# Moving the turned dV and dK tiles and the W_down^T loads on the DMA queue of a fused attention and GLU backward kernel

## The chip, the cores and the metric

The kernel runs on one core of a Trainium2 chip. Its engines are PE (TensorE, with its weight loads shown apart as PEld), DVE (VectorE), ACT (ScalarE), POOL (GpSimd) and SP (SyncE). SP does nothing here but issue DMAs, one after the other, and waits in front of each for what that DMA needs; POOL issues DMAs too, beside some arithmetic. The metric is the device time of one execution in microseconds; the figure for a kernel is the median of its runs.

## The reference

The layer is y = x + s * silu(g). With xn the layer norm of x (2048 x 576, bfloat16), s is an attention block with given keys and values, and g is a gated MLP:

```python
q = (xn @ wq).reshape(B, Sq, H, Dh)                    # H = 32 heads of Dh = 128
p = softmax(q k^T * Dh**-0.5);  o = p @ v;  s = o @ wo # Sk = 2048
h = sigmoid(xn @ w_gate) * (xn @ w_up)                 # F = 4608
g = h @ w_down
```

The kernel returns the output and the gradients of x, k, v, wq, wo, w_gate, w_up and w_down for a given grad_out. The gradients of k and v are 32 matrices of 2048 x 128 each, and those are the tiles that this change is about.

## The kernel before

The program is one straight line of stages. P is 128, NT = 16 row tiles of x, DT = 5 column tiles of D = 576 (four of 128 and one of 64).

1. Layer norm and the products with w_gate and w_up. The rows a, b and h (sigmoid, its derivative's factor, the hidden row) go to DRAM as a_d, b_d, h_d. Then h @ w_down.
2. The heads, 32 of them, to about 3610 us. Their order is written out by hand with positions. dV and dK of a head come out transposed, as 128 x 2048, and go to DRAM as dvT_d and dkT_d in pieces of 128 x 512.
3. The product of the attention rows with wo (L852), 16 row tiles. Its left operand oT is loaded and transposed by DMA into five buffers, oT0 to oT4. In its second half five pieces of W_down^T are loaded (`load_wdT`, L836), the first of three thirds: wdT0. doB and doBT, what flows back into the MLP, are made here.
4. The dh stage (L870 to L961), 18 blocks of 256 columns of F, counted by fb from 0. A block needs h_blk, a_blk and b_blk, 1024 KB each; `load_abh` (L878) loads them, two blocks ahead, into two sets of buffers: a_blk and b_blk on SP, h_blk on POOL except in block 0, where it goes on SP too. PE makes dh (L905, `make_dh`), ACT copies it out (dhc, three buffers), DVE multiplies it with a_blk and b_blk into du_blk and dg_blk, POOL stores these to DRAM, and PE goes on with dW_down (L923, `make_dwd`), then dW_up and dW_gate (L947) and the remainder of their columns (L955). Blocks 0 to 9 also load one of the ten pieces of the second and third thirds of W_down^T (wdT1, used from block 6; wdT2, used from block 12).
5. The dWo stage (L970 to L1034), eight groups of four heads (hg): dWo (L1005) from onb and ds_all, dWq (L1014, L1023) from dqb and xn_all. `load_hg` loads onb and dqb two groups ahead. `wT_loads` brings W_up^T and W_gate^T by transposing DMAs, two per group in the first five groups.
6. The last stage (L1039 to L1099), eight parts of 256 rows, counted by sbi from 0: dxn from eight passes over du, dg and dq, each loaded and transposed by DMA into cf and cq buffers (L1061), then the layer norm's backward and dx. In the last part the two dx stores are SP's, in the others POOL's.

Turning dV and dK back is spread over stages 4 to 6. The list `turns` has 64 entries, dK and dV of each head. A turn loads one 128 x 2048 matrix by a transposing DMA into a buffer named turn and stores it, 512 KB, to the output later. `turn(pool, n)` (L151) first issues the stores of all tiles loaded by the call before, then the loads of n new ones:

```python
def turn(pool, n):
    while turned:
        nc.sync.dma_start(*turned.pop(0))
    for _ in range(n):
        if turns:
            src, dst = turns.pop(0)
            t_ = pool.tile([P, NT, P], bf, name="turn")
            nc.sync.dma_start_transpose(t_[:], src)
```

Each of the three stages has its own pool of two turn buffers (4096 bytes per partition each). The dh stage turns two tiles at the end of each block (36), the dWo stage two at the end of each group (16), the last stage one at passes 1, 4 and 7 of the parts after part 0 as long as there are any: 12, the last one in part 4.

In stages 4 to 6 SP's order is the program's own (`manual_schedule`); PE, DVE, ACT and POOL are ordered by the scheduler. A DMA on SP stands behind everything that SP issues before it, and behind the wait of each of those. A buffer waits for whatever lay in the same bytes before: the pools are stacked, and the memory of one stage is that of the stage before it.

Of the kernel before, what the change touches and what calls it, by code (L numbers as in the profile page):

```python
# [9 lines left out]
bf = mybir.dt.bfloat16  # L10
# [3 lines left out]
P = 128  # L14
# [81 lines left out]
def kernel(  # L96
# [6 lines left out]
    nc = tc.nc  # L103
# [6 lines left out]
    NT = S // P  # L110
# [40 lines left out]
    def turn(pool, n):  # L151
        while turned:
            nc.sync.dma_start(*turned.pop(0))
        for _ in range(n):
            if turns:
                src, dst = turns.pop(0)
                t_ = pool.tile([P, NT, P], bf, name="turn")
                nc.sync.dma_start_transpose(t_[:], src)
                turned.append((dst, t_[:]))

# [628 lines left out]
    if True:  # L789
# [80 lines left out]
        with tc.tile_pool(name="b1o", bufs=2, reuse_waits="tile") as outp, tc.tile_pool(name="b1k", bufs=2, reuse_waits="tile") as tkp, tc.tile_pool(name="b1t", bufs=3, reuse_waits="tile") as tmpp, \  # L870
# [21 lines left out]
            for fb in range(F // FB):  # L892
                fcols = slice(fb * FB, (fb + 1) * FB)
# [44 lines left out]
                load_abh(fb + 2)  # L938
                if fb < DT * (NWD - 1):
                    load_wdT(fb % DT, 1 + fb // DT)  # L940
                turn(tkp, 2)
# [19 lines left out]
            turn(tkp, 0)  # L961
# [8 lines left out]
        with tc.tile_pool(name="c2b", bufs=1, reuse_waits="tile") as blk, tc.tile_pool(name="c2s", bufs=2, reuse_waits="tile") as sb, \  # L970
# [26 lines left out]
            for hg in range(NHG):  # L997
                cols = slice(hg * HG * P, (hg + 1) * HG * P)
                onb, dqb = held.pop(hg)
                for hl in range(HG):  # L1000
                    h = hg * HG + hl
                    accs = [ps.tile([P, 512], f32, name=f"acc{j}") for j in range(len(ncs))]
                    for st in range(NT):
                        for j, (n0, nn) in enumerate(ncs):
                            nc.tensor.matmul(accs[j][:, :nn], lhsT=onb[:, st, hl * P:(hl + 1) * P], rhs=ds_all[:, st, n0:n0 + nn],  # L1005
                                             start=(st == 0), stop=(st == NT - 1))
                    dwo = sb.tile([P, D], bf, name="dwo")
                    for j, (n0, nn) in enumerate(ncs):
                        alt.copy(dwo[:, n0:n0 + nn], accs[j][:, :nn])
                    nc.gpsimd.dma_start(out_5[h * P:(h + 1) * P, :], dwo[:])  # L1010
# [22 lines left out]
                turn(tkp, 2)  # L1033
            turn(tkp, 0)  # L1034
# [4 lines left out]
        with tc.tile_pool(name="c4c", bufs=1, reuse_waits="tile") as chp, tc.tile_pool(name="c4s", bufs=2, reuse_waits="tile") as sb, \  # L1039
# [11 lines left out]
            for sbi in range(S // SB2):  # L1051
# [7 lines left out]
                for pi, (src_d, wT, k0, KC, nm) in enumerate(passes):  # L1059
                    ch = chp.tile([P, KC, SB2], bf, name=f"cq{pi % 2}" if nm == "cq" else f"cf{pi % 3}")  # L1060
                    nc.sync.dma_start_transpose(ch[:], src_d[scol, k0 * P:(k0 + KC) * P])  # L1061
                    if sbi == 0 and pi in (1, 3, 4, 6):
                        load_wqT((1, 3, 4, 6).index(pi))
                    elif sbi and pi % 3 == 1:
                        turn(tkp, 1)
# [33 lines left out]
            turn(tkp, 0)  # L1099
# [33 lines left out]
```

## Time and profile before

| what | us |
|---|---|
| median of three runs | 5088.66 (5080.39 to 5103.23) |
| the profiled execution | 5100.3 |
| its span, first to last instruction | 5098.5 |
| PE busy in it | 4977.9 (98%) |
| the dh stage: first product of L905 to the last of L947 | 3801.5 to 4407 |
| the dWo stage: first product of L1005 | 4422.5 |
| the last stage: first product of L1072 | 4675.9 |

Lines such as "PE dh L905 <- DMA wdT<-in_B_w_down_dram: 7.9, 1, 7.9" give who waited at which line, what ended the wait, the total in microseconds, how often and the longest. "SPq" is SP's own queue of instructions, "L158 DMA_TRANSPOSE turn<-dkT_d" the issue of one DMA there. A chain or timeline line begins with its start and its length in microseconds; the length of an SP issue is how long SP was held by it, and not the transfer, whose end is its landing. A line of stretches ends with the granted share of PE's clock, the mean busy share of the 16 DMA engines (it can pass 1, since packets of two queues overlap) and GB/s.

### The profile page before, as it was taken

How to read it: one execution, taken by the hardware profiler on the slowest of the kernel's cores; microseconds unless marked ns; L12 is line 12 of the kernel's file. 1: busy time of each engine (PE TensorE's matmuls, PEld its weight loads, DVE VectorE, ACT ScalarE, POOL GpSimd, SP SyncE). 2: the span in 40 equal slices, each digit the busy share in tenths (PEclk: the TensorE clock that was granted, in tenths of full speed). 3: DMA queues.
4: the chain of work that ended last, by engine and by line, in shares of the span. 5: the costliest groups of instructions: out<-in, count | busy, mean ns of one | idle time of the engine just before them, and what ended most of it. 6: DMA issues, size and time to landing. Idle time of an engine off the chain costs nothing.

```text
span 5098.5 us, 103815 instructions
## 1 busy us (share of the span) xinstructions
PE 4977.9 (98%) x43024; PEld 3071.8 (60%) x43024; DVE 3087.7 (61%) x4821; ACT 2435.7 (48%) x3131; POOL 1484.0 (29%) x2197
## 2 busy tenths in 40 slices
PE   9999999999999999999999999999899999899999
PEld 3344666666666666666666666666457777654554
DVE  6556778878887887887888788777432222110101
ACT  5533656666666676666666667666202122100000
POOL 4322323333333333233333323322223223211000
PEclk9999999999999999999999999999999999999999
DMA  7889999999999999999999999999999999999995
GB/s 260 265 206 167 197 198 201 198 197 200 202 200 203 203 201 204 202 203 202 199 200 200 205 204 197 199 199 203 189 235 262 230 244 252 282 278 254 207 198 119
DMA packets 2855051, 1079.04 MB, mean 212 GB/s; under 512 B 2659889, under 2 KB 2782769, under 8 KB 2854577
## 3 DMA queue, kind: packets, MB, share of 16 engines
q1 hardware_dynamic: 2769312, 786.61, 87.3%
q0 software_dynamic: 85264, 285.79, 19.8%
q8 instruction: 336, 5.51, 0.4%
q14 instruction: 139, 1.13, 0.1%
HBM read 172.54 MB, written 234.55 MB: 80 GB/s over the span
## 4 chain that ended last, share of the span: by engine, by line
PE 86%; DMA 8%; issue 2%; DVE 2%; ACT 1%; POOL 1%; SPq 0%; DVEq 0%; POOLq 0%; ACTq 0%
PE acc L612 16%; PE acckv L630 15%; PE sp L552 8%; PE acc L1072 8%; PE dp L582 7%; PE accp L511 5%; PE accw L947 4%; DMA dST<-dSq 4%; PE dh L905 3%; PE acc L392 3%; PE accd L923 3%; PE acc L1005 3%; PE acc L852 2%; PE accq L1014 2%; PE acct L518 2%
## 5 line engine op out<-in xcount | busy, mean ns | idle before, releaser
L563 ACT ACTIVATE Pq<-sneg,nm 128x2048 bf16<-128x2048 bf16 x512 | 1025.0, 2002 | 182.6 <-DVE sneg L554 181.6
L585 DVE SCALAR_TENSOR_TENSOR dSq<-dp,delta,Pq 128x1024 bf16<-128x1024 f32 x608 | 774.9, 1282 | 445.9 <-PE dp L582 442.9
L612 PE MATMUL acc<-Kn,dST 128*128 128x128 bf16 x8192 | 977.0, 219 | 36.9 <-DMA dST<-dSq 36.2
L612 PEld LDWEIGHTS <-dST 128*128 128x128 bf16 x8192 | 692.3, 98 | 464.7 <-DMA dST<-dSq 57.6
L612 PE MATMUL acc<-Vn,PT 128*128 128x128 bf16 x8192 | 948.8, 219 | 11.7 <-DMA PT<-Pq 11.6
L612 PEld LDWEIGHTS <-PT 128*128 128x128 bf16 x8192 | 682.7, 98 | 428.8 <-DMA PT<-Pq 18.6
L630 PE MATMUL acckv<-Pq,dOn 128*128 128x512 bf16 x2048 | 762.9, 380 | 0.0
L630 PE MATMUL acckv<-dSq,Qn 128*128 128x512 bf16 x2048 | 758.9, 379 | 0.0
L554 DVE TENSOR_SCALAR_CACHE_REDUCE sneg<-sp,nm 128x1024 bf16<-128x1024 f32 x512 | 657.0, 1283 | 97.6 <-PE sp L552 64.8
L554 DVE TENSOR_SCALAR_CACHE_REDUCE sneg<-sp 128x1024 bf16<-128x1024 f32 x512 | 625.2, 1221 | 92.2 <-PE sp L552 82.8
L588 ACT ACTIVATE t<-dp,negdelta 128x1024 bf16<-128x1024 f32 x416 | 464.8, 1117 | 426.0 <-PE dp L582 324.5
L552 PE MATMUL sp<-KT,QT 128*128 128x512 bf16 x2048 | 610.5, 380 | 7.3 <-DVE sneg L554 7.0
L582 PE MATMUL dp<-VT,dOT 128*128 128x512 bf16 x2048 | 609.9, 379 | 0.6 <-DVE dSq L585 0.5
L592 DVE TENSOR_TENSOR dSq<-t,Pq 128x1024 bf16<-128x1024 bf16 x416 | 307.3, 739 | 0.0
L571 POOL TENSOR_TENSOR dOn<-dOn,rinv_all 128x256 bf16<-128x256 bf16 x256 | 153.8, 610 | 491.6 <-DVE dOn L42 305.4
L630 PEld LDWEIGHTS <-dOn 128*128 128x128 bf16 x2048 | 200.5, 98 | 74.5 <-issue 0.4
L630 PEld LDWEIGHTS <-Qn 128*128 128x128 bf16 x2048 | 200.5, 98 | 73.8
L511 PE MATMUL accp<-xnT,wq_h 128*128 128x512 bf16 x640 | 240.9, 381 | 2.8 <-ACT xnT L40 0.8
L947 PEld LDWEIGHTS <-xn_all 128*128 128x128 bf16 x2304 | 224.2, 98 | 27.8
L1085 DVE SCALAR_TENSOR_TENSOR junk<-dxn,xn_all 128x576 f32<-128x576 f32 x16 | 12.1, 758 | 369.3 <-ACT dxn L1080 369.3
L676 POOL DMA_DIRECT2D dq_d<-dq_n x128 | 99.1, 774 | 456.6 <-DVE dq_n L675 419.4
L1072 PEld LDWEIGHTS <-cf 128*128 128x128 bf16 x2304 | 146.3, 98 | 141.3 <-DMA cf<-dg_d 3.8
(186 smaller groups left out, 7059.2 us busy)
## 6 DMA issues: line engine op xcount, KB each, us to landing
out_dram<-turn SPq DMA_DIRECT2D x64, 512.0 KB, 4.9
h_d<-h_row POOLq DMA_DIRECT2D x48, 384.0 KB, 3.0
a_d<-a_row POOLq DMA_DIRECT2D x48, 384.0 KB, 3.5
b_d<-b_row POOLq DMA_DIRECT2D x48, 384.0 KB, 4.5
a_blk<-a_d SPq DMA_DIRECT2D x18, 1024.0 KB, 8.3
b_blk<-b_d SPq DMA_DIRECT2D x18, 1024.0 KB, 21.4
du_d<-du_blk POOLq DMA_DIRECT2D x18, 1024.0 KB, 9.6
dg_d<-dg_blk POOLq DMA_DIRECT2D x18, 1024.0 KB, 12.5
```

The source lines that it names most:

```text
L511: nc.tensor.matmul(acc[:], lhsT=w[:, i, :], rhs=(srcT if i < DL else xnT)[:, i, cs], start=(i == 0), stop=(i == DL))
L552: nc.tensor.matmul(sp[:, c * CH:(c + 1) * CH], lhsT=hs.QT[:, qs], rhs=hs.KT[:, hf * HW_ + c * CH: hf * HW_ + (c + 1) * CH], start=True, st ...
L554: nc.vector.tensor_scalar(sneg[:, hf * HW_:(hf + 1) * HW_], sp[:], -SCALE, None if hf == 0 else nm[:, hf - 1:hf], op0=ALU.mult, op1=ALU.mi ...
L563: nc.scalar.activation(Pq[:], sneg[:], AF.Exp, bias=nm[:, hf:hf + 1], scale=-1.0, accum_out=hs.rs_all[:, qt:qt + 1])
L582: nc.tensor.matmul(dp[:, c * CH:(c + 1) * CH], lhsT=hs.dOT[:, qs], rhs=hs.VT[:, hf * HW_ + c * CH: hf * HW_ + (c + 1) * CH], start=True, s ...
L585: nc.vector.scalar_tensor_tensor(dSq[:, hsl], dp[:], hs.delta[:, qt:qt + 1], Pq[:, hsl], op0=ALU.subtract, op1=ALU.mult)
L588: nc.scalar.activation(t[:], dp[:], AF.Identity, bias=hs.negdelta[:, qt:qt + 1], scale=1.0)
L592: nc.vector.tensor_tensor(dSq[:, hsl], t[:], Pq[:, hsl], op=ALU.mult)
L612: nc.tensor.matmul(bx.acc[:, j, :], lhsT=T[qt][:, kt, :], rhs=getattr(hs, rhs)[:, kt, :], start=(kt == 0), stop=(kt == NT - 1))
L630: nc.tensor.matmul(bx.acc[i][:], lhsT=getattr(hs, rhs)[:, qt, :], rhs=slabs[qt][:, k0:k0 + CH], start=(qt == 0), stop=(qt == NT - 1))
L947: nc.tensor.matmul(acc[:kd, :FB], lhsT=xn_all[:, st, d0:d0 + kd], rhs=blk_[:, st, :], start=(st == 0), stop=(st == NT - 1))
L1072: nc.tensor.matmul(accs[sl][j][:, :nn], lhsT=ch[:, kk, sl * P:(sl + 1) * P], rhs=w_[:, n0:n0 + nn], start=(pi == 0 and kk == 0), stop=(las ...
```

## The change

`turn` now loads at most one tile per call, and issues the load before the stores of what the call before loaded, so that a store stands one call, and one load, later on the queue. The calls are spread anew:

- dh stage: one at the end of each block, and one more at the start of each odd block: 27 tiles. The pool has three buffers instead of two.
- dWo stage: one at the end of each group and one after the products of each group's first head: 16 tiles as before.
- last stage: as before one at passes 1, 4 and 7 of parts 1 to 7, now used to the end: 21 tiles. The store of the last one follows the two dx stores on SP.

In the dh stage the piece of W_down^T goes on SP's queue before a_blk and b_blk of two blocks on, no longer behind them. Nothing in the heads, and no arithmetic, is changed.

```diff
--- before.py
+++ after.py
@@ -148,16 +148,15 @@
     turns = [(src[h], out[0, h].rearrange("(p t) d -> p t d", t=NT)) for h in range(H) for src, out in ((dkT_d, out_2), (dvT_d, out_3))]
     turned = []
 
-    def turn(pool, n):
-        while turned:
-            nc.sync.dma_start(*turned.pop(0))
-        for _ in range(n):
-            if turns:
-                src, dst = turns.pop(0)
-                t_ = pool.tile([P, NT, P], bf, name="turn")
-                nc.sync.dma_start_transpose(t_[:], src)
-                turned.append((dst, t_[:]))
-
+    def turn(pool, load=True):
+        old, turned[:] = list(turned), []
+        if load and turns:
+            src, dst = turns.pop(0)
+            t_ = pool.tile([P, NT, P], bf, name="turn")
+            nc.sync.dma_start_transpose(t_[:], src)
+            turned.append((dst, t_[:]))
+        for (dst, t_) in old:
+            nc.sync.dma_start(dst, t_)
 
     pers = ctx.enter_context(tc.tile_pool(name="pers", bufs=1))
     ident = pers.tile([P, P], bf, name="ident")
@@ -867,7 +866,7 @@
         pc = tc.alloc_tile_pool(name="pc", bufs=1, side="right", reuse_waits="tile")
         xn_all = pc.tile([P, NT, D], bf, name="xn_all")
         FB = min(256, F)
-        with tc.tile_pool(name="b1o", bufs=2, reuse_waits="tile") as outp, tc.tile_pool(name="b1k", bufs=2, reuse_waits="tile") as tkp, tc.tile_pool(name="b1t", bufs=3, reuse_waits="tile") as tmpp, \
+        with tc.tile_pool(name="b1o", bufs=2, reuse_waits="tile") as outp, tc.tile_pool(name="b1k", bufs=3, reuse_waits="tile") as tkp, tc.tile_pool(name="b1t", bufs=3, reuse_waits="tile") as tmpp, \
                 tc.tile_pool(name="b1r", bufs=2, reuse_waits="tile") as dblk, \
                 tc.tile_pool(name="b1l", bufs=1, reuse_waits="tile") as ldp, \
                 tc.tile_pool(name="b1ps", bufs=2, space=PSUM, reuse_waits="tile") as ps, \
@@ -890,6 +889,8 @@
             nc.sync.dma_start(xn_all[:], xn_d[:, :].rearrange("(t p) d -> p t d", p=P))
             load_abh(1)
             for fb in range(F // FB):
+                if fb % 2:
+                    turn(tkp)
                 fcols = slice(fb * FB, (fb + 1) * FB)
                 fh = slice(fb * FB % FH, fb * FB % FH + FB)
                 h_blk, a_blk, b_blk = blks.pop(fb)
@@ -935,10 +936,10 @@
                     make_dh()
                     for fl in range(FB // P):
                         make_dwd(fl)
-                load_abh(fb + 2)
                 if fb < DT * (NWD - 1):
                     load_wdT(fb % DT, 1 + fb // DT)
-                turn(tkp, 2)
+                load_abh(fb + 2)
+                turn(tkp)
                 for (blk_, out_, nm) in ((du_blk, out_7, "dwu"), (dg_blk, out_6, "dwg")):
                     stg_ = outp.tile([P, DL, FB], bf, name=nm)
                     for i, (d0, kd) in enumerate(dts[:DL]):
@@ -958,7 +959,7 @@
                 alt.copy(dwl[:], acc[:, :FB])
                 for k, out_ in enumerate((out_7, out_6)):
                     nc.gpsimd.dma_start(out_[D - KL:, fcols], dwl[k * KL:(k + 1) * KL, :])
-            turn(tkp, 0)
+            turn(tkp, False)
         pcw.release()
         pc2.release()
 
@@ -1004,6 +1005,8 @@
                         for j, (n0, nn) in enumerate(ncs):
                             nc.tensor.matmul(accs[j][:, :nn], lhsT=onb[:, st, hl * P:(hl + 1) * P], rhs=ds_all[:, st, n0:n0 + nn],
                                              start=(st == 0), stop=(st == NT - 1))
+                    if hl == 0:
+                        turn(tkp)
                     dwo = sb.tile([P, D], bf, name="dwo")
                     for j, (n0, nn) in enumerate(ncs):
                         alt.copy(dwo[:, n0:n0 + nn], accs[j][:, :nn])
@@ -1030,8 +1033,8 @@
                 load_hg(hg + 2)
                 for (dst, src, d0, kd) in wT_loads[2 * hg:2 * hg + 2]:
                     nc.sync.dma_start_transpose(dst[:, :, d0:d0 + kd], src[d0:d0 + kd, :])
-                turn(tkp, 2)
-            turn(tkp, 0)
+                turn(tkp)
+            turn(tkp, False)
 
         SB2 = min(256, S)
         FC = ldiv(FT, 12)
@@ -1062,7 +1065,7 @@
                     if sbi == 0 and pi in (1, 3, 4, 6):
                         load_wqT((1, 3, 4, 6).index(pi))
                     elif sbi and pi % 3 == 1:
-                        turn(tkp, 1)
+                        turn(tkp)
                     last = pi == len(passes) - 1
                     for kk, sl in ([(kk, sl) for sl in range(nsl) for kk in range(KC)] if last else
                                    [(kk, sl) for kk in range(KC) for sl in range(nsl)]):
@@ -1096,7 +1099,7 @@
                     dx = sb.tile([P, D], bf, name="dx")
                     nc.vector.tensor_tensor(dx[:], t2[:], got[:], op=ALU.add)
                     (nc.sync if sbi == NSB - 1 else nc.gpsimd).dma_start(o1[rows, :], dx[:])
-            turn(tkp, 0)
+            turn(tkp, False)
             assert not turns
         pc3.release()
         pc.release()
```

## The prediction

> **What bounds the kernel now.** I read the page first, then PE's waits in the stages after the heads, then the chain in order of time, then the SyncE queue's (SP's) timeline around each wait, and last the busy time by stretch. The heads, up to about 3610 us, are not touched, so only what follows them is priced.
>
> The page's first lines and PE's waits (stretches 3780:4400, 4400:4600 and 4600:4780; total us, times, longest):
>
> ```profile
> span 5098.5 us, 103815 instructions
> PE 4977.9 (98%) x43024; PEld 3071.8 (60%) x43024; DVE 3087.7 (61%) x4821; ACT 2435.7 (48%) x3131; POOL 1484.0 (29%) x2197
> PE dh L905 <- ACT dhc L909: 8.6, 3, 7.7
> PE dh L905 <- DMA wdT<-in_B_w_down_dram: 7.9, 1, 7.9
> PE acc L1005 <- DMA onb<-on_d: 13.0, 1, 13.0
> PE acc L1072 <- DMA cf<-dg_d: 3.5, 1, 3.5
> PE acc L1072 <- DMA cq<-dq_d: 2.1, 1, 2.1
> ```
>
> PE is the bound; only its few waits can be won, and all of them end on a transfer that SP issues. The chain around them (start us, us, what):
>
> ```profile
> 3966.56 8.84 PE dh L905 x80
> ...
> 3982.07 25.37 DMA wdT<-in_B_w_down_dram
> 4007.49 11.13 PE dh L905 x76
> ...
> 4124.66 27.21 DMA b_blk<-b_d
> 4153.14 4.99 PE dh L905 x30
> 4158.13 7.84 PE accd L923 x64
> ...
> 4406.82 15.60 DMA onb<-on_d
> 4422.47 17.57 PE acc L1005 x128
> ```
>
> A dh block takes PE 32.5 us (3836.48 to 3869.00). Block 6 should have begun at 3966.56+32.52 = 3999.08 and its dh ended at 4007.9; it ended at 4018.62: **10.7 us lost**, 7.9 of waiting and the rest at a slow clock (granted 0.84 over 3999:4031.5). Block 10's dh should have ended at 4148.8 (4107.40+32.52+8.84) and ended at 4158.13: **9.4 lost**. The dWo stage could have begun at 4393.61+13.97+1.87 = 4409.5; it began at 4422.47 and its first product took 17.57 instead of 15.79: **14.8 lost**. SP's timeline just before (start, us):
>
> ```profile
> 3783.31 0.38 SPq L885 DMA_DIRECT2D h_blk<-h_d  x1
> 3801.15 0.37 SPq L885 DMA_DIRECT2D a_blk<-a_d  x1
> ...
> 3948.47 13.21 SPq L158 DMA_TRANSPOSE turn<-dkT_d  x1
> 3961.72 16.56 SPq L158 DMA_TRANSPOSE turn<-dvT_d  x1
> ...
> 4402.33 3.66 SPq L153 DMA_DIRECT2D out_dram<-turn  x2
> 4406.23 0.38 SPq L994 DMA_DIRECT2D ds_all<-ds_d  x1
> ```
>
> The W_down^T piece and b_blk are late because SP was held by turns; ds_all and onb are late because the last turns end at 4406. SP's own waits add "SPq L158 <- DMA out_dram<-turn: 132.1, 24, 18.0": a load waiting for the store of the same buffer, issued just before it. But the DMA share is 1.0 to 1.2 over the whole dh stage, so much of this wait is real traffic and not free time.
>
> **The change part by part.**
>
> *Fewer tiles in the dh stage (36 to 27).* Price of a tile, load and store: the last stage shows a DMA share of 1.01 in 4829:4880 with three tiles and 0.68 in 4982:5033 with none; 0.33 of 51 us over 3 is 5.6 us. Low end: a_blk and b_blk of block 0, issued together, reached DVE 4.0 us apart (its first products with them begin at 3808.59 and 3812.57), so 1 MB is 4.0 us, and a tile moves 1 MB. High end: the pair at 3948 held SP for 30 us, 15 each. I take 5.6, the one row in which nothing but the tiles differs.
>
> *Block 6.* Its last W_down^T piece landed at 4007.45. In the changed order 6 loads and 5 stores stand ahead of it instead of 8 and 6: about 1.5 tiles, -8.4 us. It also goes ahead of a and b of its block, -8.0. Added: 4.0 for an h_blk that moves into this stage (below). It lands near 3995 against a need at 3999.1+3.9. The 10.7 go. If tiles are 4.0 it lands at 3997.
>
> *Block 10.* Its b_blk landed at 4151.87. Ahead of it now stand 12 loads and 11 stores instead of 16 and 14, 3.5 tiles, -19.6. But one more W_down^T piece is now ahead: low 1.5 us (the shortest issue), high 7.9 (the median), and I take 4.9, its median landing of 10.5 less the 5.6 of the shortest. And the h_blk of block 0 adds 4.0. So 4151.9-19.6+4.9+4.0 = 4141.2. PE comes to block 10 at 4129.2+3.9 and can go some 4 us without b (three dhc buffers and two in PSUM), to 4137.1. Some 4 us late, and 2 for the slow clock: 6 of the 9.4 stay, **3.4 won**. From block 11 no W_down^T piece is left, and SP gains.
>
> *The third turn buffer.* It is 4096 bytes per partition, and everything allocated above it moves up. In the built program h_blk of block 0 then lies on oT0, which the last product of the stage before (L852, to about 3801.1) still reads. Before, h_blk was issued at 3783.31 and only a_blk waited for that. Now h, a and b all go after 3801.1. With h first, b comes one transfer (4.0) and one issue (0.4) later. PE reached the first product of L947 8.1 us after b (3812.35 to 3820.48); of the dwd products that stand between, 25 instead of 29 are left then, 0.5 us less: **+3.9**. Low end 0 (h hidden under the first dh blocks), high end 12, were h to hold b up by the 21.4 us less 10.8 that b's median landing has over this one. SP, ACT and POOL queue behind it, and all move by as much.
>
> *Start of the dWo stage.* After the last a/b loads only 4 loads and 5 stores are left instead of 6 and 6. Before, a of block 17 went at 4350 and SP was free at 4406. Two tiles less are 11 us, and in the seven blocks from 11 on, half a tile less per block brings SP forward by 2.8 each: it is free near 4375 for ds_all. onb waits for PE's last dwd, 15.8 us before the stage ends; its median landing is 11.1, so it is there. Late next is dqb: it waits for the dwl stores and was issued at 4415.78, 6.3 us after PE's end; it is needed 15.8 after, and takes 8.5 (the shortest) to 13.6 (the median). Price 0 to 4, I take 1, for ds_all and onb no longer run beside it. The new turn behind it on SP waits for PE's accl only, long ended. **-13.8**.
>
> *In the dWo stage* the number stays 16; one tile moves to the stage's head, and a load waits for the store issued one step before it, as now. SP's cover is its waits on PE (29.9 us at L992 in all). 0, between -2 and +2.
>
> *The last stage (12 to 21).* The nine tiles fall into parts 5 to 7. Parts 1 to 4 carry the same three per part with PE at 51.00 of 51:
>
> ```profile
> 4829.00:4880.00 51.00, 51.00 (x418) 26.21 (x416) 6.30 (x16) 1.78 (x8) 2.15 (x4) 1.00 1.01 207
> 4982.00:5033.00 51.00, 51.00 (x419) 26.46 (x418) 6.29 (x16) 1.78 (x8) 2.15 (x4) 1.00 0.68 147
> ```
>
> The cover is SP's slack on PE, 10.7 us in the first of these stretches and 21.2 in the second. 0 on PE; without the cover a late cf costs 3.5 and, as at onb, about 2 of slow clock. The last store, though, now stands behind the two dx stores: the last dx issue begins at 5095.63 and lands 1.8 later; the turn's store is issued 0.33 behind it and takes 2.8 (the shortest) to 4.9 (the median): +1.3 to +3.4. Nothing else is in flight then, so I take the low end: **+1.4**.
>
> **Sum.** 3.9-10.7-3.4-13.8+1.4 = **-22.6 us**. The profiled execution took 5100.3 (span 5098.5 and 1.8 around it): 5077.7. It is 11.6 above the median of the three runs, 5088.66; the same difference on the median gives **5066.1**, -0.44%.
>
> One rule makes the tiles cheaper. The Trainium skill, page "Advanced Engine Details and Errata", section "X-Bar Transpose (TRN2)", says that transposing transfers are as fast as plain ones. By it a tile would be 4.0 us (an estimate from a and b above) and a W_down^T piece of 0.375 MB 1.5: block 10 then comes 5.6 less 3.4, some 2.2 us, later than priced, and the sum would be -20.4. The trace's windows (5.6) disagree.
>
> **The rivals.**
>
> *Both dh waits go and block 10 is free* (the queue is the limit, not the engines: 132.1 us of SP's waits fall away). For it: a_blk lands in 6.2 us at its best and 24.2 at its worst, the same megabyte, by what POOL's du, dg and h do beside it. Against: the DMA share never falls below 0.97 there, so a transfer moved is a transfer somewhere else. It gives 6 us more: 5060.1. A rule beside it: "DMA: Bandwidth & Descriptors", section "Queues, rings and completion order" of the Trainium skill, says that each DMA engine takes turns between the queue rows that have work; a tile less on SP's row would then free more than its own time while POOL's row is full. The trace's 6.2 to 24.2 us agree with it.
>
> *The traffic stays in the way*: turns that meet POOL's three 1 MB transfers are slow whatever their number (12 to 17 us each at 3948 and again at 4262, against a median of 2.6). Then blocks 6 and 10 lose what they lose now: 14.1 more, 5080.2. Against: fewer turns meet them.
>
> *Slower than before*: the nine late tiles hold cf or cq back. If each costs 3.5+2 us, that is 49.5: 5115.6. It decides once SP's 10.7 us of slack per part are used up; the parts that carry three tiles now speak against it.
>
> **How the numbers follow.** Forecast 0.42 (its own range 5060 to 5073), block 10 free 0.26, traffic stays 0.23, slower 0.09. The range takes in the first three with the ends of the unknown costs (start to +12, dqb 3, clock): 5050 to 5092. A measurement of this kernel can tell about 0.5% from no change, here 25.4 us. Below 5063.2 lie nearly all of the second case and a quarter of the first: 0.34; above 5114 most of the last: 0.08; between, 0.58.
>
> **What would show it.** In the profile after: PE's wait on wdT gone and onb's gone or under 2; a wait of a few us on dhc or b_blk near block 10; h_blk of block 0 issued by SP after the last L852 product instead of 18 us before, and PE idle some 4 us there; ds_all issued before PE's last dwd; parts 5 to 7 of the last stage at a DMA share near 1 with PE full; a turn store as the last transfer. I am wrong if the dh stage has new waits on a_blk or wdT, if dqb waits for more than 3 us, or if cf does after part 4.

## The result, and the profile after

The changed kernel takes 5123.01 us (median of 20 runs, 5098.3 to 5165.2) against 5104.43 for the kernel before (20 runs beside them): the ratio is 1.0046, 95% interval 1.0024 to 1.0068. It is slower by a little under half a per cent, where 5066 and a small gain had been forecast. A later comparison on another chip gave 1.0027 (1.0002 to 1.0052).

The page of the profiled execution (5136.24 us) begins:

```profile
span 5134.5 us, 103068 instructions
PE 4950.8 (96%) x42270; PEld 3077.3 (60%) x43024; DVE 3088.9 (60%) x4821; ACT 2437.8 (47%) x3131; POOL 1483.9 (29%) x2197
```

PE's waits of the changed kernel, first over the dh stage (3826:4460), then up to the first parts of the last stage (4460:4780); total us, times, longest:

```profile
PE dh L906 <- issue: 16.7, 3, 8.5
PE dh L906 <- ACT dhc L910: 3.6, 2, 3.4
PE accd L924 <- DMA h_blk<-h_d: 3.6, 1, 3.6
PE accd L924 <- issue: 2.9, 3, 1.4
...
PE acc L1075 <- DMA cf<-dg_d: 5.6, 2, 4.8
PE acc L1075 <- DMA cf<-du_d: 5.5, 2, 3.6
```

The rows that were to go are gone: no wait on wdT in the dh stage, none on onb at the start of the dWo stage. New are 16.7 us of "issue" in the dh product (PE stands and nothing that the profile follows holds it), 2.9 more in dwd, and 11 us on cf where there were 3.5. The chain of the changed kernel shows the places:

```profile
4096.85 7.40 issue
4104.25 9.24 PE dh L906 x69
...
4186.97 22.95 DMA b_blk<-b_d
4211.19 6.09 PE dh L906 x30
...
4249.26 8.49 issue
...
4700.51 8.44 DMA cf<-du_d
...
4726.56 6.30 DMA cf<-dg_d
```

Two of the stops lie in the middle of a dh product whose operands are all there. The DMA view of the changed kernel over 4090:4110 says what was late (queue, packets, MB, share of 16 engines):

```profile
DMA packets 2662, 2.57 MB, mean 129 GB/s; under 512 B 2166, under 2 KB 2166, under 8 KB 2660
...
q8 instruction: 1, 0.02, 2.0%
```

and the same 20 us of the kernel before:

```profile
DMA packets 3050, 4.67 MB, mean 233 GB/s; under 512 B 1717, under 2 KB 2059, under 8 KB 3049
...
q8 instruction: 1, 0.02, 0.3%
```

The instruction queue q8 carries PE's program: it has 336 packets and 5.51 MB on the page, so 16.4 KB a packet, and 5.51 MB are 64 bytes for each of PE's 43,024 products and as many weight loads. The one packet here took 2.0% of 16 x 20 us = 6.4 us instead of 0.3%, or 1.0. By the trace's packets it ran from 4096.46 to 4102.80, and PE went on at 4104.25. Before it PE had begun some 454 instructions since the packet before; at the second stop some 491, and PE went on 1.3 us after that packet's end. In the whole dh stage of this trace of the kernel before the longest such step is 414, and nothing stops at it. In the dh stages of all 20 traces there are 18 stops on "issue" of over 1 us, and each ended 1.2 to 1.7 us after such a packet, with 426 to 507 instructions begun since the packet before; steps up to 479 also passed without a stop of that length. The Trainium skill, page "Advanced Engine Details and Errata", section "ISA Cache", gives cache lines of 16 KB or 256 instructions, and only two of them; the packets' size and the 426 to 507 agree with that, and not with the 128 KB that it also gives for TensorE. So PE's code was late, by the same DMA engines that carry the data. Only one of the two packets was itself slow; the one at the second stop took 1.2 us and had started late, and no run shows what held it back.

SyncE's (SP's) timeline shows what was in flight beside the first of them. One stretch of the changed kernel (start us, us that SP was held, what):

```profile
4046.00 19.24 SPq L156 DMA_TRANSPOSE turn<-dkT_d  x1
...
4065.91 2.99 SPq L836 DMA_TRANSPOSE wdT<-in_B_w_down_dram  x1
4068.95 0.58 SPq L884 DMA_DIRECT2D a_blk<-a_d  x1
4069.63 3.62 SPq L884 DMA_DIRECT2D b_blk<-b_d  x1
4073.29 18.63 SPq L156 DMA_TRANSPOSE turn<-dvT_d  x1
4092.03 0.53 SPq L159 DMA_DIRECT2D out_dram<-turn  x1
4092.65 17.48 SPq L156 DMA_TRANSPOSE turn<-dkT_d  x1
```

Once per block POOL moves du, dg and h, 3 MB, within some 20 us. A transposing load that falls into this burst holds SP 15 to 20 us; one between bursts 2 to 5; one that meets only a part of it something between. In these 64 us three turns were held. The turn issued at 4073.29 landed after 36.2 us, and the late instruction packet lies within that time.

The place on SP's own queue counts as well: two of these three turns stand right behind b_blk. In the four traces of the changed kernel that the table below goes by, 64 of the 108 turns of the dh stage stand there; 40 of them held SP 15 us or longer, and the shortest held it 7.0. Of the other 44, 6 held it so long. In the four traces of the kernel before no turn stands right behind b_blk, and 10 of 144 held SP 15 us or longer.

Because single executions scatter, both kernels were traced three more times. Stage times in us from PE's instructions; "c1" is the first attention-output product (L851 here, L852 before), which no edit touches:

| | end of c1 | dh | idle | dWo | idle + last | tail | c1 to end |
|---|---|---|---|---|---|---|---|
| before, four traces | 3801 to 3820 | 608.3, 621.6, 608.8, 614.1 | 13.0, 15.4, 12.0, 7.7 | 253.1 to 254.6 | 415.4, 419.0, 418.5, 414.7 | 7.1 | mean 1303.0 |
| changed, four traces | 3806 to 3826 | 621.7, 605.6, 608.2, 599.5 | 0.1, 0, 7.3, 0 | 252.5 to 254.0 | 425.0, 435.8, 423.5, 424.8 | 8.4 | mean 1299.6 |
| change of the mean | +8.5 | -4.4 | -10.2 | -0.4 | +10.4 | +1.3 | -3.4 |

What was won before the dWo stage is given back at the start of the last, and the dh stage wins little. By these means the stages behind c1 are level, and the four traces don't show where the timed 14 to 19 us are lost. The traced executions of the kernel before took 5114 us in the mean, 10 above the median of its 20 runs, and those of the changed kernel 5119, 4 below the median of its own: the traces are 5 us apart. The unchanged work up to the end of c1 ended anywhere from 3801 to 3830 us in the 20 traces of all kernels, so four traces of each can't settle it. The timed experiments below tell more of the cause than this table.

### The profile page after: what moved, and what is told of

It reads as the page before. It is cut to its first block, busy times and chain, and to the rows that moved or that the text cites. A ratio compares the mean times of both kernels' runs of the same rounds, so it can differ in the third digit from the quotient of the medians.

```text
span 5134.5 us, 103068 instructions
## 1 busy us (share of the span) xinstructions
PE 4950.8 (96%) x42270; PEld 3077.3 (60%) x43024; DVE 3088.9 (60%) x4821; ACT 2437.8 (47%) x3131; POOL 1483.9 (29%) x2197
## 3 DMA queue, kind: packets, MB, share of 16 engines
q8 instruction: 336, 5.51, 0.4%
## 4 chain that ended last, share of the span: by engine, by line
PE 85%; DMA 8%; DVE 2%; issue 2%; ACT 1%; SPq 1%; POOL 0%; DVEq 0%; ACTq 0%; POOLq 0%; another core or an unknown queue 0%
PE acc L611 17%; PE acckv L629 14%; PE sp L551 8%; PE acc L1075 7%; PE dp L581 7%; PE accp L510 5%; PE accw L948 5%; DMA dST<-dSq 3%; PE dh L906 3%; PE acc L391 3%; PE accd L924 3%; PE g_ps L294 2%; PE acc L1006 2%; PE u_ps L294 2%; PE acct L517 2%
## 5 line engine op out<-in xcount | busy, mean ns | idle before, releaser
L611 PE MATMUL acc<-Kn,dST 128*128 128x128 bf16 x8192 | 978.3, 219 | 51.1 <-DMA dST<-dSq 36.6
L611 PE MATMUL acc<-Vn,PT 128*128 128x128 bf16 x8192 | 948.8, 219 | 18.6 <-DMA PT<-Pq 12.2
L629 PE MATMUL acckv<-Pq,dOn 128*128 128x512 bf16 x1887 | 704.9, 380 | 1.9
L629 PE MATMUL acckv<-dSq,Qn 128*128 128x512 bf16 x1891 | 700.9, 380 | 1.7
L581 PE MATMUL dp<-VT,dOT 128*128 128x512 bf16 x1951 | 589.2, 380 | 2.4 <-DVE dSq L584 0.3
L510 PE MATMUL accp<-xnT,wq_h 128*128 128x512 bf16 x579 | 219.1, 383 | 4.4 <-ACT xnT L40 0.8
```

What stands on the lines that cost most here:

```text
L510: nc.tensor.matmul(acc[:], lhsT=w[:, i, :], rhs=(srcT if i < DL else xnT)[:, i, cs], start=(i == 0), stop=(i == DL))
L581: nc.tensor.matmul(dp[:, c * CH:(c + 1) * CH], lhsT=hs.dOT[:, qs], rhs=hs.VT[:, hf * HW_ + c * CH: hf * HW_ + (c + 1) * CH], start=True, s ...
L611: nc.tensor.matmul(bx.acc[:, j, :], lhsT=T[qt][:, kt, :], rhs=getattr(hs, rhs)[:, kt, :], start=(kt == 0), stop=(kt == NT - 1))
L629: nc.tensor.matmul(bx.acc[i][:], lhsT=getattr(hs, rhs)[:, qt, :], rhs=slabs[qt][:, k0:k0 + CH], start=(qt == 0), stop=(qt == NT - 1))
```

## The experiments

Each was built to undo or do one part. The ratios, with their 95% intervals, are against runs of the kernel before on the same chip; "dh" and the other stages are as in the table, and come from one traced execution of each kernel.

**The turns gated.** In the dh stage a load waits for the store of the tile before it, as it did before the change.

```diff
-  tc.tile_pool(name="b1k", bufs=3, ...) as tkp
+  tc.tile_pool(name="b1k", bufs=1, ...) as tkp   # and a dummy of two tiles
   turn(tkp): 
+    store of the old tile, and then
     load of the next
-    store of the old tile
```

> The changed kernel with one thing different in the dh stage: each turn load goes into the one buffer (two more buffers' worth of room kept as a dummy, so every other tile lies where it did), and the store of the tile before it is issued first, so that a load waits until that store has landed. Counts (27, 16, 21), places in the program and the W_down^T order stay. Theory P (place): in the changed kernel a turn load is issued right behind a_blk and b_blk without waiting, runs beside POOL's du, dg and h transfers, takes 30 us and more to land six times, and PE's own instruction packets and b_blk come late behind it; gated, few loads should take over 25 us, PE's idle time in the dh stage that nothing explains (16.7 us in the changed kernel's trace) should be under 5, the dh stage about 595 to 608 us instead of 621.7, and the whole 10 to 25 us faster than the changed kernel, near 1.000 of before. Theory Q (order): W_down^T ahead of a_blk and b_blk makes b late; this run changes nothing of that, dh about 620, ratio about 1.004. Theory L (layout): the late first h_blk moves everything; unchanged here, ratio about 1.004.

The ratio is 1.0042 (1.0020 to 1.0064). The stage did what P said: dh 598.9, median turn landing 5.9 us (22.0 in the changed kernel), one turn over 25 us instead of seven, one PE stop of 3.9. The total did not: SP waited 150.5 us for its own stores, came late to the end of the stage, and onb was 12.4 us late again. Gating moves the loss and does not remove it.

**The old order of the loads.**

```diff
+ load_abh(fb + 2)
  if fb < DT * (NWD - 1):
      load_wdT(fb % DT, 1 + fb // DT)
- load_abh(fb + 2)
  turn(tkp)
```

> The changed kernel with a_blk, b_blk and h_blk issued ahead of the W_down^T piece again, as in the kernel before; all else as changed. Theory Q (order): b_blk lands 2 to 8 us earlier in blocks 1 to 10, the dh stage is 8 to 13 us shorter than the changed kernel's 621.7, ratio to before about 1.002. Theory P (place of the turns): the turn still goes right behind the loads, now behind the W_down^T piece too; dh 610 to 630, stalls of PE without a shown cause still over 10 us, ratio about 1.004. Theory L: about 1.004.

It took 5088.54 against 5097.63, a ratio of 0.9994 (0.9971 to 1.0016): more was won back than Q expected. dh is 591.9, with nothing but the first h_blk and 0.2 us on dhc in PE's waits over it:

```profile
PE accd L924 <- DMA h_blk<-h_d: 3.1, 1, 3.1
PE pt L797 <- DVE doB L861: 0.2, 1, 0.2
PE dh L906 <- ACT dhc L910: 0.2, 1, 0.2
```

SP's timeline of this kernel is a clockwork:

```profile
4113.94 0.38 SPq L884 DMA_DIRECT2D a_blk<-a_d  x1
4114.41 1.55 SPq L884 DMA_DIRECT2D b_blk<-b_d  x1
4116.01 20.16 SPq L836 DMA_TRANSPOSE wdT<-in_B_w_down_dram  x1
4136.27 2.95 SPq L156 DMA_TRANSPOSE turn<-dkT_d  x1
4139.26 0.58 SPq L159 DMA_DIRECT2D out_dram<-turn  x1
4146.46 0.36 SPq L884 DMA_DIRECT2D a_blk<-a_d  x1
```

a_blk goes when DVE has finished dg_blk, every 32.5 us. The W_down^T piece, now right behind b_blk, takes the burst's 20 us, which nobody waits for, and the turn goes in the quiet after it. From block 10 on, where no piece is left, a turn takes that place and is held as long; the step stays.

**The turn buffers above the blocks**, so that h_blk0 and a_blk0 are clear of oT0.

```diff
- tile_pool("b1k", bufs=3) as tkp, ... tile_pool("b1l", bufs=1) as ldp
+ tile_pool("b1l", bufs=1) as ldp, tile_pool("b1k", bufs=3) as tkp
```

> The changed kernel with the three turn buffers allocated above the h, a and b blocks instead of below them, so that neither h nor a of block 0 lies on the attention-output tile that the stage before reads last; all else as changed. Theory L (layout): h, a and b of block 0 are there when the stage begins, the 3.6 us wait for h_blk goes, and everything behind it on SyncE and POOL moves up: 4 us less by the sum of the prediction, up to 13 if the whole loss of the dh stage began there; ratio to before 1.002 to 1.004. Theory P: 4 us less and no more, the 30 us turn loads and PE's stalls stay; ratio about 1.004.

The ratio is 1.0030 (1.0007 to 1.0052). The wait for the first h_blk is gone and no more: dh 598.2 with stops of 3.0 and 4.8 us, five turns over 25 us, onb 4.6 late.

**No turns in the dh stage** (27 tiles of the two outputs left out).

```diff
+ del turns[:27]
- if fb % 2: turn(tkp)
- turn(tkp)
```

> The changed kernel without the 27 turns of the dh stage: these tiles of dV and dK are not turned at all, so that their part of the two outputs is left unwritten; the dWo and last stages turn 16 and 21 as changed. It bounds what the turns of the dh stage cost. Theory P: without them PE's instruction packets and the blocks come in time, dh near 18 x 32.5 + 4 to 8 at the start = 590 to 595 us, about 27 us less than the changed kernel's 621.7, ratio to before about 0.999; the start of the dWo stage still costs nothing. Theories Q and L: the late b_blk or late first h_blk cost even without turns, dh 605 to 615. If dh stays near 620, it was not the turns at all.

The ratio is 0.9979 (0.9958 to 1.0001) and dh 593.8, with SP in step and W_down^T still first. So the order by itself does the dh stage no harm, and the 27 turns by themselves neither (591.9 with them in the old order). The two together do.

**The old order in block 0 only, and in all blocks but block 0.**

```diff
+ if fb == 0: load_abh(fb + 2)      # the other kernel: if fb:
  load_wdT(...)
+ if fb: load_abh(fb + 2)           # the other kernel: if fb == 0:
- load_abh(fb + 2)
```

The kernel with the old order in block 0 only:

> The changed kernel with the old order (h, a, b ahead of W_down^T) in block 0 only; in blocks 1 to 9 W_down^T goes first as changed. Theory S (start): one transposing load per block falls into POOL's burst of du, dg and h and is held 15 to 20 us; SyncE has room for one of these per 32.5 us block but not for two. With W_down^T ahead of a and b in block 0 it is held 16.8 us, a and b go 38 us late, and from then on two loads per block meet a burst and SyncE stays late. On time in block 0, it should stay on time: a_blk issued every 32.5 us as soon as DVE has dg_blk, dh stage 590 to 596 us, no PE gap over 3 us beyond the first h_blk, whole 25 to 35 us below the changed kernel, ratio to before 0.998 to 1.000. Theory O (order in every block): nine of ten pieces are still ahead, dh 612 to 625, ratio 1.003 to 1.005.

The kernel with the old order in all blocks but block 0:

> The changed kernel with the old order (h, a, b ahead of W_down^T) in blocks 1 to 9 and W_down^T first in block 0 alone. Theory S: SyncE is late from block 0 on and stays late for many blocks, dh 605 to 625 with PE gaps, ratio 1.002 to 1.005. Theory O: nine of ten pieces are behind again, so dh 592 to 596, ratio 0.998 to 1.001. If SyncE gets back on time within two or three blocks, dh is between, 595 to 603: then the place in block 0 starts the lateness and the place in the later blocks keeps it.

Neither theory stands as written. With only block 0 put right, a_blk of blocks 2 to 4 went 23, 64 and 94 us after the end of c1 (22, 62 and 83 in the old order), that of block 5 at 154 instead of 114; dh 602.0, 1.0026 (0.9996 to 1.0056). With only block 0 wrong, a_blk of block 2 went at 38 and SP never found its step: dh 616.1, turns over 25 us six times, 1.0006 (0.9979 to 1.0034). So one misplaced piece can throw SP off, in block 0 or later, and once off it stays off for long. These are single executions, and the one with dh 616.1 took 5134.57, nearly the slowest of its 12 runs: how often a piece in block 0 alone does this isn't shown.

**The changed kernel a second time.**

> The changed kernel itself once more, for a second trace. If SyncE is late again in the dh stage by the order of the program and not by chance, its a_blk loads again leave the 32.5 us step, four or more turn loads again take over 25 us to land, dh is again 605 to 625 us and PE stops once or more with nothing shown that it waits for, though at other places. If the first trace was chance, dh is near 592 to 600.

This execution took 5118.09. SP is off step again (a_blk 38, 95, 122, 163 us after c1), and dh is 605.6. This time 9.6 of PE's waits were on dhc, 3.3 on h_blk0 and only 1.4 were "issue": which stop it is differs, that SP is off step does not. New was 11.8 us of cf before the last stage.

**A first combination**: old order, buffers above, 31 tiles in dh, 12 in dWo, 21 in the last.

```diff
- if fb % 2:            turn(tkp)
+ if fb % 2 or fb >= 10: turn(tkp)
- if hl == 0:                     turn(tkp)   # dWo stage
+ if hl == 0 and hg < NHG - 2:    turn(tkp)
- turn(tkp)                                   # end of a head group
+ turn(tkp, hg < NHG - 2)
```

> A candidate to beat both: the changed kernel with h, a, b ahead of W_down^T, the turn buffers above the h, a and b blocks, 31 tiles in the dh stage (one more in blocks 10, 12, 14 and 16, where no W_down^T piece is left), 12 in the dWo stage with none behind the last two head groups, and 21 in the last. Against the run with the old order alone: 3 to 4 us less at the start of the dh stage (no wait for h_blk), and 5 to 10 less at the start of the last stage (SyncE is free for the first two cf loads some 15 to 20 us earlier). If both hold, 5075 to 5081 us, ratio 0.996 to 0.998. If the four more tiles make SyncE late before the dWo stage, onb waits again up to 12 us and nothing is won on the old order alone, 0.999 to 1.001.

It took 5097.58 against 5105.16, 0.9986 (0.9955 to 1.0017), which isn't told apart from before. Its trace has what was wanted (dh 587.1, first part of the last stage, from its first product to its last, 59.4, 1269.2 from c1 to the end), and onb 4.4 late.

**The kernel before, again.**

> The kernel before itself, for a second trace. The prediction summed the waits of one trace: 10.7 us in block 6, 9.4 in block 10, 14.8 at the start of the dWo stage. If these belong to the kernel, they come again at the same places: dh 605 to 611 us, then 12 to 14 idle, 1295 to 1300 us from the end of the first attention-output product to the end. If the two in the dh stage were chance, PE stops in other blocks or hardly at all, dh 590 to 603, and 1280 to 1292 from there to the end; only the dWo wait comes again.

> The same again, for a third trace, to see by how much the stages of one kernel differ between executions. The heads, whose code no change touches, ended at 3665.5 us in the first trace of this kernel and at 3661 to 3691 in the ten others so far; if that is chance and not the kernel, these two are spread over that range as well.

Two of the three priced losses belong to the kernel. In all four of its traces PE waits for a W_down^T piece in block 6 (7.9, 21.0, 1.6 and 3.2 us) and for onb (13.0, 15.4, 12.0 and 7.7). The wait in block 10 is in the first trace alone; the others wait on dhc in block 5 or 12, or not at all. In the second trace PE's waits are:

```profile
PE dh L905 <- DMA wdT<-in_B_w_down_dram: 21.0, 1, 21.0
PE acc L1005 <- DMA onb<-on_d: 15.4, 1, 15.4
PE accd L923 <- issue: 6.3, 4, 3.3
```

In the third it is 8.2 on dhc, 1.6 on wdT and 12.0 on onb, and PE stops on "issue" for 4.4 us here too: a turn meets a burst in this kernel as well, only less often (2 or 3 of 36 turns held SP 15 us or longer, against 10 to 12 of 27 in the changed kernel). The heads ended at 3668.8 and 3664.6.

**Only the numbers of tiles**, in the kernel before.

```diff
- turn(tkp, 2)
+ turn(tkp, 2 - fb % 2)
```

> The kernel before with nothing but the numbers of tiles changed, to the 27, 16 and 21 of the changed kernel: two turns after even blocks and one after odd ones, still both stores first, still h, a, b ahead of W_down^T, two buffers. By the prediction's price of a tile (5.6 us of SyncE's road) SyncE is earlier by 25 us at block 10 and by 50 at the end: both waits of the dh stage go, onb is in time, 20 to 30 us less, ratio 0.994 to 0.997. If a gated pair costs SyncE little (it lands in 5 us in the quiet part of a block), the number does not matter much: dh 595 to 605, the dWo wait shrinks by 5 us at most, ratio 0.998 to 1.000.

The ratio is 0.9991 (0.9967 to 1.0014); dh is 595.2, there is no onb wait, and it is 1276.0 us from c1 to the end. In this trace the numbers alone give what the prediction asked of the whole change (27 us under the mean of before); the medians show 11.5 of it, 5095.3 against 5106.81, and the interval doesn't exclude that nothing is won.

**Only the order**, in the kernel before.

```diff
+ if fb < DT * (NWD - 1): load_wdT(fb % DT, 1 + fb // DT)
  load_abh(fb + 2)
- if fb < DT * (NWD - 1): load_wdT(fb % DT, 1 + fb // DT)
  turn(tkp, 2)
```

> The kernel before with nothing but the order of two calls changed: W_down^T ahead of h, a and b, as in the changed kernel; 36, 16 and 12 tiles in pairs, two buffers. By the prediction the piece that block 6 waits for comes 8 us sooner, so that at least that wait goes: ratio 0.997 to 0.999. By the reading of the runs so far, a W_down^T piece that goes first meets POOL's burst and holds a and b behind it, and the turns behind a and b are held too: dh 612 to 630, ratio 1.001 to 1.005.

The ratio is 1.0006 (0.9984 to 1.0028), dh 591.0, and onb 18.4 late. My reading missed: with the turns still in pairs behind their stores, W_down^T first does not hurt the stage.

**On one chip side by side.**

> The changed kernel again, timed beside the next three on one chip. If it loses in the dh stage and at the start of the last stage, it is again 1.003 to 1.006 of before, and its trace has dh 603 to 625 and 2 to 12 us idle before the last stage. If the loss was that of the one chip it was first timed on, 0.998 to 1.002. If the loss lies in the heads and not in what was changed, the heads end after 3672 us in this trace as in its first two, while the stages behind them take what the kernel before takes (1297 to 1316).

> The changed kernel with h, a, b ahead of W_down^T once more. If the order is the cause, it is again 20 to 35 us under the changed kernel's run of this call, a_blk is issued every 32.5 us from block 3 on, dh is 590 to 596, nothing idle before the dWo stage. If the first result was chance, it is within 10 us of the changed kernel.

The changed kernel took 5116.01 (1.0027, 1.0002 to 1.0052) and the one with the old order 5101.69 (0.9982, 0.9962 to 1.0002): 14 us by the medians, 23 by the ratios, where 20 to 35 had been expected. On the two chips used before, the same two kernels stood at 1.0046 and 0.9994. Both times the new order of the loads costs the changed kernel some 0.5%. The old order had dh 592.2 and its step; the changed kernel 608.2, with ten of 27 turns over 25 us and one stop of 12.6, which ended 1.3 us after an instruction packet. But the old order too had 11.9 us of waiting for cf before the last stage.

**The dWo stage's turns in pairs**, old order in dh.

```diff
- if hl == 0: turn(tkp)
  ... end of the head group:
- turn(tkp)
+ stores of the old pair, loads of the next two
```

> The run with the old order, and in the dWo stage the turns as in the kernel before: both stores and then two loads at the end of each head group, none at its start; 27, 16 and 21 tiles as before. If the single turns, each behind the store of the one before, hold SyncE at the end of the dWo stage, the first cf load is issued 8 to 12 us earlier against the end of that stage, nothing is idle ahead of the last stage (2.2 us), its first part takes 60 to 63 us instead of 65.1, and the whole is 4 to 7 us under the run with the old order alone. If the first part's waits are SyncE's own load of cf and wqT pieces, within 2 us of it.

It took 5082.96 against 5107.92, 0.9964 (0.9944 to 0.9984): a little faster than the kernel before and the changed kernel. From the old order alone (0.9982) the times don't tell it apart; the traces do. SP's timeline of the kernel without pairs (abh_first_again), where the dWo stage ends at 4664.8:

```profile
4621.89 3.10 SPq L993 DMA_DIRECT2D dqb<-dq_d  x1
4625.33 14.02 SPq L156 DMA_TRANSPOSE turn<-dkT_d  x1
4639.44 0.54 SPq L159 DMA_DIRECT2D out_dram<-turn  x1
4643.06 2.44 SPq L156 DMA_TRANSPOSE turn<-dvT_d  x1
...
4665.82 11.22 SPq L1064 DMA_TRANSPOSE cf<-du_d  x2
```

and of the one with pairs, where it ends at 4669.1:

```profile
4612.55 2.00 SPq L1003 DMA_DIRECT2D dqb<-dq_d  x1
4614.64 7.81 SPq L164 DMA_DIRECT2D out_dram<-turn  x2
...
4630.07 1.96 SPq L168 DMA_TRANSPOSE turn<-dvT_d  x1
4632.07 3.44 SPq L168 DMA_TRANSPOSE turn<-dkT_d  x1
...
4658.15 8.62 SPq L1072 DMA_TRANSPOSE cf<-du_d  x2
```

The first cf goes 11.0 us before the end of the stage instead of 1.0 after it. From the last dqb load to cf it is about the same in both (44 and 46 us); the 12 us were lost earlier: with a turn between every two steps SP comes to that last load 43 us before the end of the stage instead of 57. The first part of the last stage takes 62.6 against 66.7, and the idle time before it is 0 against 11.9. The other traces agree: in the eleven with 16 single turns in the dWo stage the first cf goes from 6.6 us before its end to 1.0 after it, and "idle + last" is 422 to 436; in the seven with pairs it goes 10.2 to 15.9 before, and "idle + last" is 415 to 420.

These lines show one thing more. POOL moves no du, dg or h in the dWo stage, and still the turn right behind dqb held SP for 14.02 us. So it was with all 126 transposing loads that stand right behind dqb in the 20 traces: 10.7 to 19.3 us. A large load of SP's own, right ahead, holds a transposing load without any burst.

**The combination, its extra tiles in blocks 4, 6, 8 and 10.**

```diff
- if fb % 2 or fb >= 10:           turn(tkp)
+ if fb % 2 or fb in (4, 6, 8, 10): turn(tkp)
```

> The candidate again with its four extra dh tiles in blocks 4, 6, 8 and 10 instead of 10, 12, 14 and 16, so that SyncE is free before the dWo stage. If the four tiles made onb late (4.4 us), that goes: dh 586 to 590, no wait for onb, first part of the last stage 60, from the end of the first attention-output product to the end 1262 to 1268 us, 10 to 14 under the run with the old order alone, ratio 0.995 to 0.997. If the extra tiles throw SyncE off its step in the middle of the stage, dh 595 or more, ratio 0.999 or more.

It took 5082.23, 0.9961 (0.9936 to 0.9986), level with the pairs. Its profiled execution (5123.82) is the slowest of its runs and shows the other face: dh 622.9, with stops of 7.9 and 10.1 us that each ended 1.5 to 1.7 us after an instruction packet. With a tile more in some blocks the step seems less safe; this one execution is all that shows it.

**A fourth trace of each.**

> The kernel before, a fourth trace. If the unchanged part is really shorter in this kernel, the first attention-output product again ends by 3809 us; if it is chance, it ends anywhere from 3800 to 3830 (the range of the other sixteen traces). Behind it: a wait for a W_down^T piece or for ACT in blocks 4 to 7, dh 600 to 622, 12 to 15 us idle before the dWo stage, 1295 to 1316 in all.

> The changed kernel, a fourth trace. If the unchanged part is really longer in it, the first attention-output product ends after 3814 us again; if that is chance, anywhere from 3800 to 3830. Behind it: dh 605 to 622 with PE stopped at least once with nothing shown that it waits for, 0 to 8 idle before the dWo stage, 2 to 12 before the last, 1300 to 1310 in all.

The end of c1 is at 3820.1 in the kernel before and at 3806.3 in the changed one, the other way round than in the first traces: the time ahead of the changed stages looks like chance. The changed kernel's dh was 599.5 here, with stops of 2.1 and 2.8 only, outside the expected 605 to 622; PE's waits of the kernel before hold 12.6 us on dhc, 4.7 on "issue" and again 3.2 on a W_down^T piece.

## Why the prediction was wrong

*The base.* The measured time lies 57 us above the forecast. The forecast was 22.6 us below a median of three runs, 5088.66. Twenty runs have 5104.43. That alone is 16 us; the other 41 are the sum, -22.6 forecast and +18.6 measured.

*The start, +3.9:* right. h_blk0 goes at 3825.75, when c1 has ended at 3825.6, and PE waits 3.6 (3.1 to 3.9 in the other kernels of that layout, nothing with the buffers above).

*Block 6, -10.7, and block 10, -3.4:* the waits named did go, in all four traces, but the stage won 4.4 and not 10.2, start included. (The wait in block 10 is no witness: the kernel before has it in one trace of four. Nor can the table tell 4.4 from 10.2, with single traces 13 and 22 us apart; the timed runs show the failure.) This is the step that failed: SP was costed as a row of transfers, each with its price (a tile 5.6, a piece 4.9), so that what stands ahead of b decides. What decides is where a transposing load stands: whether it falls into POOL's burst, and what is right ahead of it on SP's queue. The price of a turn is 2 to 5 us of SP between bursts and 15 to 20 in one, and right behind b_blk the cheapest of the changed kernel's cost 7; "6 loads and 5 stores instead of 8 and 6" says nothing of that. W_down^T first, with a turn issued straight behind b, puts two transposing loads into bursts in some blocks; SP falls off its 32.5 us step, turns land after 13 to 22 us in the median instead of 6 to 9, and PE then stops for whatever comes late: h_blk, dhc by b_blk, its own code. That the two parts only hurt together is shown by undoing either: dh is 591.9 and 592.2 without the order, 593.8 without the turns and 598.9 with the turns gated, and the ratio falls from 1.0046 and 1.0027 to 0.9994 and 0.9982 without the order and to 0.9979 without the turns. How much of a hold is the burst's and how much b_blk's own, right ahead, no run was built to part. The rival "the traffic stays in the way" had the right mechanism, turns that meet POOL's transfers, and the wrong place: it kept the old losses, when new ones took their place. The sentence against it, "fewer turns meet them", was wrong: 10 to 12 of 27 turns were held 15 us or longer, where 2 or 3 of 36 had been.

*The start of the dWo stage, -13.8:* right in three traces of four (0.1, 0 and 0 idle), 7.3 in the one where SP was latest; -10.2 in the mean. dqb never held anything.

*The dWo stage, 0:* right for the stage (253.3 against 253.7), wrong for what follows. "SP's cover is its waits on PE" was the cover of PE in this stage. The single turns used it up: behind the last dqb load the first of them held SP 14 us, where the pairs have their two stores, 8. So cf came late, and the last stage begins and runs through its first part 10.4 us later. This is the second step that failed; putting the pairs back took 4 to 16 us off the same place.

*The last stage, 0 for nine more tiles, and +1.4 for the last store:* right. Two stretches of the changed kernel, in parts 5 and 6, which carry added tiles:

```profile
4974.00:5025.00 51.00, 50.58 (x410) 26.34 (x418) 6.29 (x16) 1.83 (x10) 2.19 (x5) 1.00 1.04 213
5025.00:5076.00 51.00, 50.53 (x410) 26.43 (x417) 6.29 (x16) 1.83 (x9) 2.19 (x5) 1.00 0.98 209
```

The DMA share is near 1, PE is full (this trace has records of 410 products where the prediction's stretches have 418), no part after the first exceeds 51.1 us in any of the four traces, and a turn's store is the last transfer (tail 8.4 against 7.1). The rival of the nine late tiles was wrong: cf does come late, but in part 0 and not in parts 5 to 7. That its 5115.6 lies nearest to the measured time is luck.

With the old order and the dWo pairs, the same numbers of tiles do give what was forecast for the change: 0.9964, or some 18 us (25 by the medians). The gain was there; two of the edits that came with the numbers spent it. Of the two the order is shown by the times on two pairs of runs; the single turns of the dWo stage are shown by the traces, and by the times only together with the order.

## What to carry to other kernels

On a queue that issues in order, look at what a transposing load meets when it goes, and what stands right ahead of it, and not only at how many stand ahead: keep it from standing right behind a large load that is itself slow, place it behind one that may be held, in the quiet part of the block, and leave the burst to a load that nobody waits for. Check every stage that follows a rearranged one for the point at which the queue is free; a cover that is used up in one stage is missed at the start of the next. And trace a kernel more than once before pricing a single wait: here the dh stage alone scattered by 13 and 22 us between four executions of the two kernels.

## What the runs showed of the hardware

A matmul stream can stop for its own code. PE's program comes by the same DMA engines as the data, in 16.4 KB packets of 1.0 us (median); beside turns that took 22 to 36 us in flight one such packet took 6.4 us and others came late, and PE stood up to 12.6 us in the middle of a product with its operands present. The profile has no name for it but "issue"; the instruction queue's row in the DMA view is where to look. The Trainium skill, page "DMA: Bandwidth & Descriptors", section "Queues, rings and completion order", has each DMA engine take turns between the rows with work; no run here shows whether that, or something else, stretched the one packet to 6.4 us. No "issue" stop of over 1 us is in the dh stage of the five traces in which SP kept its step.

A transposing load can be held by what stands right ahead of it on its own queue. Right behind dqb, 126 of them held SP 10.7 to 19.3 us in a stage without POOL's burst; right behind b_blk, the turns of the changed kernel held it 7.0 to 22.5 us.
